# Batch 1's K and Q loaded and cast before the first feed-forward chunk, with a denser order for its attention

## The chip, the core and the metric

The kernel runs on one core of one Trainium2 chip. The time is the device time of one launch in microseconds; three runs of the kernel before gave 375.75 to 376.08, median 375.94. The engines are named as the profile names them: PE (TensorE, matrix products; PEld is its weight load), DVE (VectorE), ACT (ScalarE), POOL (GpSimd) and SP (SyncE, which here only issues DMAs). Each engine runs its own instructions in the order of the program and waits for the others by semaphores. ACTq and SPq in the profile are the sequencers of ACT and SP issuing DMAs.

## What is computed

Selective attention with a decay, then a feed-forward layer with a gate, in float32 from end to end in the reference:

```python
def _attn_ref(q, k, v, s) -> np.ndarray:
    B, H, S, D = q.shape
    scale = 1.0 / np.sqrt(D)
    scores = scale * np.matmul(q, k.transpose(0, 1, 3, 2))
    causal = np.triu(np.ones((S, S), dtype=bool), k=1)
    s_pos = np.maximum(s, 0.0)
    cum = np.cumsum(s_pos, axis=-1)
    bias = -(cum[:, :, :, None] - cum[:, :, None, :])
    scores = np.where(causal, -1000000000.0, scores + np.minimum(bias, 0.0))
    scores = scores - np.max(scores, axis=-1, keepdims=True)
    attn = np.exp(scores)
    attn = attn / (np.sum(attn, axis=-1, keepdims=True) + 1e-09)
    return np.matmul(attn, v).astype(np.float32)

def _moe_ref(x, w_gate, w_val, w_out, rms_g) -> np.ndarray:
    rms = np.sqrt(np.mean(x * x, axis=-1, keepdims=True) + 1e-06)
    xn = x / rms * rms_g
    g = xn @ w_gate
    silu = g * (1.0 / (1.0 + np.exp(-g)))
    val = xn @ w_val
    return (silu * val @ w_out).astype(np.float32)
```

Q, K and V have 8 batches, 8 heads, 576 rows and 64 columns; the gate, value and output weights are 512 x 1536, 512 x 1536 and 1536 x 512. The attention's output, 8 batches of 576 rows with 512 columns (8 heads of 64), is the input x of the feed-forward layer: 4608 tokens.

## The kernel before

**Feed-forward.** The 4608 tokens are cut into nine chunks of 512, whatever the batches; `ffn(c)` does one. For each of twelve blocks fb of 128 hidden columns, PE makes the gate product (L668, four matrix products into a bank psF), ACT takes the tanh of it into T (L671), PE makes the value product (L677), DVE makes U from T and the gate (L680) and one block later Ht from U and the value (L673; the last one is L685). Then four output tiles of twelve products each (L690) are copied by ACT (L695) and stored by SP (L697). psF has four buffers, T two.

**Attention.** A batch has nine score steps S(b, kb, g), key block kb of 128 keys, head group g of four heads (kb = 4 is the short last block with all eight heads), and ten value steps AV(b, qb, g), query block qb. Ahead of them K and Q must be cast to bf16 and be transposed:

- `load_kq` and `load_kq_tail` load K (w = 0) or Q (w = 1) of a batch into kq32, rows 0 to 511 and the last 64. kq32 is one buffer for each of K and Q, so the load of batch 1 waits for all casts of batch 0.
- `cast` writes part r of five (r = 4 is the tail) to kqn. For batch 2 and 3 the casts of both, from batch 4 on those of Q, are POOL's, planned by `casts`.
- `t_step` transposes two heads (hp) of K or Q on PE (L184) and copies the result to kqT, on ACT (L192) or DVE (L190); `tail_step` does the tails of all heads (L200, L205 to L209). From batch 2 on Q is transposed by DMA on SP (`kq_dma`, L171), from batch 4 on K too.
- `s_step` makes the scores on PE (L250) and their exponentials on ACT (L274), half of them in the next slot; POOL puts zeros above the diagonal (L283).
- `av_step` multiplies by V on PE (L300, L306), then DVE takes the reciprocal of the sums (L313) and scales (L315). With g = 1 the squares are summed, on DVE (L325) or ACT (L321), and POOL makes the row's factor in two instructions (L328, L331). g = 0 uses the bank psAV, g = 1 of batches from 1 on psT; there is one buffer of each.
- `x_scale` (L338, DVE) applies the factor three slots after AV(b, qb, 1). The result is transposed into xnT by DMA on SP (L348), or for batch 0 and for (1, 3) by PE (`xt_step`, L357, into psT).
- `check_mag` and `check_max` keep the largest magnitude of the cast K and Q (L369, then L375 for each half), for a test at the end which chooses between this path and a general one.

**Order.** There are no loops on the chip here; Python writes the instructions out in an order that it plans. A prologue, written by hand, does batch 0 up to query block 3 and ends with the transpose of x(0,3), which the first chunk needs. Every chunk then has 36 slots: `step()` is called after each gate group and each value group (slots 1 to 23), after the last Ht (24) and after each four output products (25 to 36). A slot takes at most one entry from each side queue (`act_side`, `pool_side`, `dve_side`; `v_side` in odd slots), all first in, first out, and then emits one S with a transpose of batch 1, or up to two of an x transpose, an AV and a transpose. `can_s`, `can_av`, `can_t` and `can_xt` say when, by the slots at which the inputs were emitted. In slots called bare, `pool_side` and `v_side` stand still; in chunk 0 these are 30 to 33.

`later(queue, lag, fns)` puts work into a side queue for `lag` slots ahead. For batch 1 the casts of K are in `act_side` and `pool_side`, those of Q in `dve_side` and `pool_side`. `check(0, (0,))` puts the check of batch 0's K into `dve_side`; its Q is checked in the prologue, after the last x transpose. The checks allow `casts(2)` to overwrite kqn.

The tokens of chunk 1 reach into batch 1, query block 3: x(1,3) is the last thing that chunk 1 waits for, and its transpose stands in chunk 0, in slot 34.

Of the kernel before, what the change touches and what calls it, by code (L numbers as in the profile page):

```python
# [26 lines left out]
def kernel(  # L27
# [76 lines left out]
    def psF16():  # L104
        return pp.tile([128, 8, 128], BF16, name="psF16", tag="F", bufs=4)
# [10 lines left out]
    def psT():  # L116
        return pp.tile([128, 8, 128], BF16, name="psT", tag="T", bufs=1)
# [5 lines left out]
    def load_kq(eng, b, w, h0=0, h1=H):  # L123
        src = k if w == 0 else q
        eng.dma_start(
            out=kq32[:, w, h0:h1, 0:256],
            in_=src[b, h0:h1, 0:512, :].rearrange("h (p r) d -> p h (r d)", r=4))

    def load_kq_tail(eng, b, w):
        src = k if w == 0 else q  # L130
        eng.dma_start(
            out=kq32[0:64, w, :, 256:320],
            in_=src[b, :, 512:576, :].rearrange("h p d -> p h d"))

    def cast(eng, b, w, r0, r1, h0=0, h1=H):
        o = kqn[:, b % 2, w, r0:r1, h0:h1, :]
        i = kq32[:, w].rearrange("p h (r d) -> p r h d", d=D)[:, r0:r1, h0:h1, :]
        if eng is nc.scalar:
            eng.activation(out=o, in_=i, func=AF.Copy)
        else:  # L140
            eng.tensor_copy(out=o, in_=i)
# [193 lines left out]
    def x_scale(b, qb):  # L335
        n = rows(qb)
        col = b * NSC + qb
        nc.vector.scalar_tensor_tensor(  # L338
            out=xs_sb[0:n, (b * NSC + qb) % NX, :], in0=x_sb[0:n, (b * NSC + qb) % NX, :],
            scalar=al_all[0:n, col:col + 1], in1=g_row[0:n], op0=ALU.mult, op1=ALU.mult)  # L340
# [68 lines left out]
    def later(queue, lag, fns):  # L409
        t = slot[0] + lag  # L410
        queue.extend((lambda: slot[0] >= t, f) for f in fns)
# [6 lines left out]
    def check(b, ws=(1, 0)):  # L418
        t = slot[0] + (8 if b >= KB else 0)

        def when(w):
            if b < 2:
                return slot[0] % 2 and chunk[0] == b
            return phase() >= 25 and slot[0] >= t and (w == 0 or ready(0, "cast", b, 1))
        dve_side.extend((lambda w=w: when(w), f) for w in (ws if b < KB else (0, 1)) for f in (
            lambda w=w: check_mag(b, w), lambda: check_max(0), lambda: check_max(1),
            lambda w=w: done.__setitem__(("check", b, w), slot[0])))

    def phase():

        return slot[0] - first[0]
# [57 lines left out]
    def do_t(key, **kw):  # L489
        b, hp, w = key  # L490
        if hp == "tail":
            tail_step(b)
            done["T", b] = slot[0]
            after_tail(b)
        else:
            if b == 1:
                kw["dve"] = w == 1 and hp > 1
                if hp % 2:
                    kw["pT"] = psF16()
            t_step(b, hp, w, **kw)  # L500
        done["T", b, hp, w] = slot[0]
        last["T"] = slot[0]
# [21 lines left out]
    def do_xt(key, pX=None):  # L524
        b, qb = key
        xt_step(b, qb, pX)
        done["XT", b, qb] = slot[0]
        last["T"] = slot[0]
# [13 lines left out]
    def can_s():  # L542
        if not s_seq or not slot_free():
            return False
        b, kb, g = s_seq[0]
        if b == 1 and (phase() < 24 and phase() % 2 == 0 or kb == 4 and at("AV", 1, 3, 1) > slot[0]):
            return False
        due = SLOTS * ((b * S + kb * 128) // DM) - (26 if b == 1 else 18 if b < 4 else 14)
        if slot[0] - last["S"] < (4 if slot[0] < due - 24 else 3 if slot[0] < due else 2):
            return False  # L550
        if b >= XB:
            return all(ready(5, "X", b, 1, c) for c in (kb, min(kb + 1, 4))) and (
                ready(5, "X", b, 0, kb) if b >= KB else ready(3, "T", b) if kb >= 3 else
                all(ready(3, "T", b, hp, 0) for hp in (2 * g, 2 * g + 1)))
        if kb >= 3 and not ready(3, "T", b):
            return False
        if kb == 4:
            return True
        return all(ready(3, "T", b, 2 * g + j, w) for j in (0, 1) for w in (0, 1))

    def can_av(clear=False):
        if not av_seq:
            return False
        b, qb, g = av_seq[0]
        if slot[0] - last["AV"] < (1 if (b, qb) == (1, 3) else 2):
            return False
        if b > 0 and g == 1 and slot[0] - last["T"] < 3 and not clear:
            return False
        if b > 1 and not ready(8, "V", b):
            return False  # L570
        if qb > 0 and not ready(5, "S", b, qb - 1, g):
            return False
        prev = b * NSC + qb - NX
        if prev >= 0 and at("XT", prev // NSC, prev % NSC) > slot[0]:
            return False
        return ready(4 if (b, qb) == (1, 3) else 5, "S", b, qb, g)
# [22 lines left out]
    def step(bare=False):  # L599

        slot[0] += 1
        while pending:
            pending.pop(0)()
        moved = False
        if scaled[0] < len(x_list):
            b, qb = x_list[scaled[0]]
            if ready(3, "AV", b, qb, 1):
                x_scale(b, qb)
                scaled[0] += 1
                if not by_pe(b, qb):  # L610
                    assert xt_seq[0] == (b, qb)
                    xt_dma(*xt_seq.pop(0))
                    done["XT", b, qb] = slot[0] + 4
                    moved = True
        run_side(act_side)
        if not moved and x_seq and slot[0] - last["X"] >= 2:
            b, w, c = x_seq[0]
            if (ready(2, "cast", b, 1) and ready(1, "S", b - 2, 4, 0)
                    and (w == 1 or ready(7, "K", b, c))):
                x_seq.pop(0)  # L620
                kq_dma(b, w, c)
                done["X", b, w, c] = last["X"] = slot[0]
                if b >= KB and (w, c) == (0, NSC - 1) and b + 2 < B:
                    casts(b + 2)
        bare = bare or chunk[0] == 0 and 30 <= phase() <= 33
        if slot[0] % 2 and not bare:
            run_side(v_side)
        if not bare:
            run_side(pool_side)
        run_side(dve_side)  # L630
        if can_s():
            pending.append(do_s(s_seq.pop(0)))
            if t_seq and t_seq[0][0] == 1 and can_t():
                do_t(t_seq.pop(0))
            return
        n = 0
        if can_xt():
            do_xt(xt_seq.pop(0))
            n += 1
        if can_av():  # L640
            do_av(av_seq.pop(0))
            n += 1
        if n < 2 and t_seq and can_t():
            do_t(t_seq.pop(0))
# [126 lines left out]
    with tc.manual_schedule():  # L771
# [28 lines left out]
        def piece(w, g, r, eng):  # L800
            cast(eng, 0, w, r, r + 1, 4 * g, 4 * g + 4)
# [4 lines left out]
        def s_first(kb, g, pair=None):  # L806
            do_s((0, kb, g), pair)()
# [25 lines left out]
        do_t((0, 3, 0), pT=psF16(), dve=True)  # L833
        for r in range(4):
            piece(1, 1, r, DVE)
        s_first(2, 0)
        for w in (0, 1):
            cast(POOL, 0, w, 4, 5)
        do_t((0, 2, 1), pT=psT(), dve=True)
        do_t((0, 3, 1), pT=psF16(), dve=True)  # L840
        do_av((0, 0, 0))
# [10 lines left out]
        s31 = do_s((0, 3, 1), pairF())  # L852
        s31(False)
        do_av((0, 0, 1), psT32())

        for w in (0, 1):
            nc.vector.memset(kq32[0:1, w, 0, 0:1], 0.0)
            load_kq(nc.sync, 1, w)
            load_kq_tail(nc.sync, 1, w)
        s30.mask()  # L860
        do_av((0, 1, 1), act=True)
        s31.mask()
# [14 lines left out]
        do_xt((0, 2), psF16())  # L877
        warm(2)
        x_scale(0, 3)
        do_xt((0, 3), psF16())  # L880
        check_mag(0, 1)
        check_max(0)
        check_max(1)
        done["check", 0, 1] = 0

        def done_cast(w):
            done["cast", 1, w] = slot[0]
        later(act_side, 1, [lambda r=r: cast(ACT, 1, 0, r, r + 1) for r in range(4)])
        later(pool_side, 1, [lambda: cast(POOL, 1, 0, 4, 5)])
        later(pool_side, 3, [lambda: done_cast(0)])  # L890
        later(pool_side, 4, [lambda: cast(POOL, 1, 1, 2, 3),
                             lambda: (cast(POOL, 1, 1, 3, 4), done_cast(1)),
                             lambda: cast(POOL, 1, 1, 4, 5)])
        later(dve_side, 3, [lambda r=r: cast(DVE, 1, 1, r, r + 1) for r in (0, 1)])
        later(v_side, 0, [
            lambda: load_v(1, 0), lambda: load_v(1, 1), lambda: load_v(1, 2),
            lambda: nc.gpsimd.dma_start(out=wout_sb,
# [2 lines left out]

        loads(2, 1, later, 14)
        loads(2, 0, later, 18)
        check(0, (0,))
        check(1)
        casts(2)

# [192 lines left out]
```

## Time and profile before

| what | value |
|---|---|
| three runs, median (range) | 375.94 us (375.75 to 376.08) |
| the profiled execution | 375.92 us, its span 374.2 us |
| granted clock of PE | 0.998 |
| first gate product of chunk 0, of chunk 1 | 32.12, 76.35 us |
| prologue's ACT, DVE and POOL busy, 20 to 30 us | 7.50, 6.83 and 6.56 of 10 us |
| first S of batch 1 (slot 11), first AV (slot 16) | 45.83, 52.46 us |
| AV(1,3,1) (slot 30), transpose of x(1,3) (slot 34) | 68.47, 74.15 us |
| load of batch 1's K, Q (rows 0 to 511): issue, to landing | 23.17 and 6.3; 24.35 and 9.0 us |

The span runs from the first to the last instruction; the time of the execution holds some 1.7 us more around it. All the times of single instructions are from the span's start. A row of a group has the line, the engine, the operation, the tile it writes and those it reads; x12 is a count; behind it stand the busy time, the mean length and the idle time of the engine ahead of it, with what ended that. Successive instructions of one engine overlap by up to 0.08 us in the records, so what an instruction costs its engine is the distance from its start to the next one's.

### The profile page before, as it was taken

What the parts mean: (1) busy time and instruction counts of PE and PEld (TensorE: products, weight loads), DVE (VectorE), ACT (ScalarE), POOL (GpSimd) and SP (SyncE); (2) the same over time, 40 slices, a digit from 0 to 9 for tenths busy, and PEclk for the clock granted to TensorE, in tenths of its full rate; (3) what the DMA queues carried; (4) which work ended last, traced back from release to release, by engine and by line L of the source; (5) the groups of instructions that cost most, each with busy time, mean ns of one, the idle gap of its engine ahead of it and who ended that gap; (6) DMA issues with size and microseconds to landing.
All of it is one profiled execution on the core that took longest, in us unless ns stands there. A gap on an engine that the chain in (4) does not pass through costs nothing. (4 is left out here: it accounts for less than half of the span.)

```text
span 374.2 us, 6937 instructions
## 1 busy us (share of the span) xinstructions
PE 347.0 (93%) x2356; PEld 161.4 (43%) x2356; DVE 279.7 (75%) x525; ACT 239.8 (64%) x626; POOL 174.4 (47%) x277
## 2 busy tenths in 40 slices
PE   1867899899999999899999999999999999999993
PEld 1443444454444444344444444444444444444441
DVE  6758988589887878788889897785488548837830
ACT  3777787547877597786777776777677744323321
POOL 5865734974846575779756825522322310000000
PEclk9999999999999999999999999999999999999999
DMA  8999999899997599959999997992210230020012
GB/s 230 189 227 237 146 196 220 123 204 225 155 168 105 53 195 165 159 55 204 149 162 225 136 107 152 120 67 44 96 26 14 44 105 3 0 84 31 0 44 76
DMA packets 125626, 46.22 MB, mean 124 GB/s; under 512 B 104912, under 2 KB 120784, under 8 KB 125584
## 3 DMA queue, kind: packets, MB, share of 16 engines
q0 software_dynamic: 59920, 11.80, 42.7%
q1 hardware_dynamic: 53040, 24.33, 34.6%
q10 hardware_dynamic: 12624, 9.59, 10.5%
q8 instruction: 20, 0.33, 0.4%
q14 instruction: 22, 0.18, 0.2%
HBM read 38.16 MB, written 9.44 MB: 127 GB/s over the span
## 5 line engine op out<-in xcount | busy, mean ns | idle before, releaser
L274 ACT ACTIVATE E<-psS,biasK 128x256 bf16<-128x256 f32 (+3 forms) x352 | 114.9, 415 | 19.7 <-PE psS L250 18.1
L668 PE MATMUL psF<-xnT,wg_sb 128*128 128x512 bf16 x432 | 111.1, 379 | 2.4 <-DMA xnT<-xs_sb 1.3
L677 PE MATMUL psF<-xnT,wv_sb 128*128 128x512 bf16 x432 | 111.1, 379 | 0.1
L690 PE MATMUL psF<-wout_sb,Ht 128*128 128x512 bf16 x432 | 102.3, 379 | 0.0
L283 POOL TENSOR_SCALAR_AFFINE_SELECT E<-E 128x512 bf16<-128x512 bf16 x72 | 52.2, 725 | 93.7 <-ACT E L274 92.8
L671 ACT ACTIVATE T<-psF 128x512 f32<-128x512 f32 x108 | 64.3, 597 | 42.1 <-PE psF L668 38.7
L680 DVE SCALAR_TENSOR_TENSOR U<-T,psF 128x512 bf16<-128x512 f32 x108 | 73.6, 682 | 21.9 <-ACT T L671 21.8
L673 DVE TENSOR_TENSOR Ht<-U,psF 128x512 bf16<-128x512 bf16 x99 | 67.7, 684 | 7.5 <-PE psS L250 0.5
L668 PEld LDWEIGHTS <-wg_sb 128*128 128x128 bf16 x432 | 38.7, 98 | 46.9 <-issue 8.0
L677 PEld LDWEIGHTS <-wv_sb 128*128 128x128 bf16 x432 | 38.6, 98 | 42.8 <-issue 4.6
L690 PEld LDWEIGHTS <-Ht 128*128 128x128 bf16 x432 | 38.7, 98 | 42.1 <-issue 2.3
L338 DVE SCALAR_TENSOR_TENSOR xs_sb<-x_sb,al_all,g_row 128x512 bf16<-128x512 bf16 (+1 forms) x40 | 32.8, 822 | 16.1 <-POOL al_all L331 14.5
L695 ACT ACTIVATE osb<-psF 128x512 f32<-128x512 f32 x36 | 21.4, 595 | 33.7 <-PE psF L690 29.4
L321 ACT ACTIVATE xs_sb<-x_sb 128x512 bf16<-128x512 bf16 (+1 forms) x36 | 22.9, 639 | 22.3 <-DVE x_sb L315 22.2
L175 POOL DMA_DIRECT2D v_sb<-in_v_dram x40 | 35.3, 883 | 0.4 <-issue 0.3
L375 DVE TENSOR_TENSOR acc<-acc,mag 128x1280 bf16<-128x1280 bf16 x32 | 29.4, 936 | 0.4
L250 PE MATMUL psS<-kqT 64*128 64x256 bf16 (+2 forms) x304 | 26.8, 262 | 1.6 <-ACT E L274 1.5
L306 PEld LDWEIGHTS <-E 128*128 128x128 bf16 x320 | 22.3, 99 | 13.3 <-POOL E L283 3.4
L328 POOL TENSOR_SCALAR al_all<-ss_all 128x1 f32<-128x1 f32 (+1 forms) x40 | 11.1, 277 | 28.5 <-ACT xs_sb L321 23.0
L300 PEld LDWEIGHTS <-E 128*128 128x128 bf16 x256 | 20.6, 99 | 7.9 <-DVE x_sb L315 0.6
L331 POOL TENSOR_TENSOR al_all<-al_all,mhalf 128x1 f32<-128x1 f32 (+1 forms) x40 | 22.2, 556 | 3.3
L250 PEld LDWEIGHTS <-kqT 64*128 64x128 bf16 x320 | 10.4, 97 | 29.9 <-issue 28.6
(94 smaller groups left out, 278.8 us busy)
## 6 DMA issues: line engine op xcount, KB each, us to landing
out_dram<-osb SPq DMA_DIRECT2D x36, 256.0 KB, 2.3
kq<-in_q_dram ACTq DMA_DIRECT2D x6, 1024.0 KB, 9.5
v_sb<-in_v_dram POOLq DMA_DIRECT2D x32, 128.0 KB, 7.2
kq<-in_k_dram ACTq DMA_DIRECT2D x2, 1024.0 KB, 10.6
kqn<-in_k_dram POOLq DMA_DIRECT2D x16, 128.0 KB, 5.6
wg_sb<-in_moe_w_gate_dram POOLq DMA_DIRECT2D x2, 768.0 KB, 7.3
wv_sb<-in_moe_w_val_dram POOLq DMA_DIRECT2D x2, 768.0 KB, 10.3
wout_sb<-in_moe_w_out_dram POOLq DMA_DIRECT2D x1, 1536.0 KB, 14.1
```

The source lines that it names most:

```text
L175: nc.gpsimd.dma_start(out=v_sb[0:n, b % 2, c, :, 0:64], in_=v[b, :, c * 128:c * 128 + n, :].rearrange("h p d -> p h d"))
L250: nc.tensor.matmul(pair[par][:, j * W:j * W + M], lhsT=kT, rhs=qT, start=(j == 0), stop=(j == nj - 1))
L274: nc.scalar.activation(out=eo, in_=ei, func=AF.Exp, scale=0.125, bias=biasK[:, kb, bh:bh + 1])
L283: nc.gpsimd.affine_select(out=Ev[:, :, 0:nq], in_=Ev[:, :, 0:nq], pattern=[[0, nh], [1, nq]], compare_op=ALU.is_ge, fill=0.0, base=0, chan ...
L338: nc.vector.scalar_tensor_tensor(out=xs_sb[0:n, (b * NSC + qb) % NX, :], in0=x_sb[0:n, (b * NSC + qb) % NX, :], scalar=al_all[0:n, col:col ...
L375: nc.vector.tensor_tensor(out=acc[:, sl], in0=acc[:, sl], in1=mag[:, sl], op=ALU.max)
L668: nc.tensor.matmul(Gp, lhsT=wg_sb[:, cc, fs], rhs=xnT[:, cc, x0:x0 + DM], start=(cc == 0), stop=(cc == CC - 1))
L671: nc.scalar.activation(out=T, in_=Gp, func=AF.Tanh, scale=0.5)
L673: nc.vector.tensor_tensor(out=Ht[:, fb - 1, :], in0=pend[0], in1=pend[1], op=ALU.mult)
L677: nc.tensor.matmul(Vp, lhsT=wv_sb[:, cc, fs], rhs=xnT[:, cc, x0:x0 + DM], start=(cc == 0), stop=(cc == CC - 1))
L680: nc.vector.scalar_tensor_tensor(out=U, in0=T, scalar=1.0, in1=Gp, op0=ALU.add, op1=ALU.mult)
L690: nc.tensor.matmul(Op, lhsT=Ht[:, fb, tb * 128:(tb + 1) * 128], rhs=wout_sb[:, fb, :], start=(fb == 0), stop=(fb == FB - 1))
```

## The change

It concerns batch 1 and the checks of batch 0:

- The loads of batch 1's K and Q are issued by SP some way earlier in the prologue: the main parts behind the DVE casts of batch 0's Q, the tails behind POOL's casts of batch 0's tails.
- At the end of the prologue, K is cast in two parts by DVE and two by ACT, Q in four parts by DVE. The two tails stay on POOL, in slots 1 and 4. The casts that POOL, ACT and DVE had in slots 1 to 4 are gone, and the planner is told that the casts are done (slot -1).
- The prologue no longer checks batch 0's Q: both checks of batch 0 are in `dve_side`, from slot 9 on.
- The copies of all Q transposes of batch 1 are DVE's; those of the first two were ACT's.
- S of batch 1 may come every second slot from the start (`due` is 36 slots ahead, not 26). AV of batch 1 may follow one slot after another from slot 22 on; before, that was so for query block 3 alone.
- The bare slots of chunk 0 are 27 to 30.

```diff
@@ def check(b, ws=(1, 0)) @@
             if b < 2:
-                return slot[0] % 2 and chunk[0] == b
+                return slot[0] % 2 and chunk[0] == b and slot[0] >= 9
@@ def do_t(key, **kw) @@
             if b == 1:
-                kw["dve"] = w == 1 and hp > 1
+                kw["dve"] = w == 1
@@ def can_s() @@
-        due = SLOTS * ((b * S + kb * 128) // DM) - (26 if b == 1 else 18 if b < 4 else 14)
+        due = SLOTS * ((b * S + kb * 128) // DM) - (36 if b == 1 else 18 if b < 4 else 14)
@@ def can_av(clear=False) @@
-        if slot[0] - last["AV"] < (1 if (b, qb) == (1, 3) else 2):
+        if slot[0] - last["AV"] < (1 if b == 1 and slot[0] > 21 else 2):
@@ def step(bare=False) @@
-        bare = bare or chunk[0] == 0 and 30 <= phase() <= 33
+        bare = bare or chunk[0] == 0 and 27 <= phase() <= 30
@@ the prologue @@
         for r in range(4):
             piece(1, 1, r, DVE)
+        for w in (0, 1):
+            DVE.memset(kq32[0:1, w, 0, 0:1], 0.0)
+            load_kq(nc.sync, 1, w)
         s_first(2, 0)
         for w in (0, 1):
             cast(POOL, 0, w, 4, 5)
+            load_kq_tail(nc.sync, 1, w)
...
-        for w in (0, 1):
-            nc.vector.memset(kq32[0:1, w, 0, 0:1], 0.0)
-            load_kq(nc.sync, 1, w)
-            load_kq_tail(nc.sync, 1, w)
         s30.mask()
...
         x_scale(0, 3)
+        cast(DVE, 1, 0, 2, 3)
+        cast(DVE, 1, 0, 3, 4)
+        cast(ACT, 1, 0, 0, 1)
         do_xt((0, 3), psF16())
-        check_mag(0, 1)
-        check_max(0)
-        check_max(1)
-        done["check", 0, 1] = 0
-
-        def done_cast(w):
-            done["cast", 1, w] = slot[0]
-        later(act_side, 1, [lambda r=r: cast(ACT, 1, 0, r, r + 1) for r in range(4)])
+        cast(ACT, 1, 0, 1, 2)
+        for r in range(4):
+            cast(DVE, 1, 1, r, r + 1)
+        done["cast", 1, 0] = done["cast", 1, 1] = -1
         later(pool_side, 1, [lambda: cast(POOL, 1, 0, 4, 5)])
-        later(pool_side, 3, [lambda: done_cast(0)])
-        later(pool_side, 4, [lambda: cast(POOL, 1, 1, 2, 3),
-                             lambda: (cast(POOL, 1, 1, 3, 4), done_cast(1)),
-                             lambda: cast(POOL, 1, 1, 4, 5)])
-        later(dve_side, 3, [lambda r=r: cast(DVE, 1, 1, r, r + 1) for r in (0, 1)])
+        later(pool_side, 4, [lambda: cast(POOL, 1, 1, 4, 5)])
...
-        check(0, (0,))
+        check(0)
         check(1)
```

## The prediction

> **What bounds the kernel now.** I read first the page's busy row and the table of windows.
>
> ```profile
> PE 347.0 (93%) x2356; PEld 161.4 (43%) x2356; DVE 279.7 (75%) x525; ACT 239.8 (64%) x626; POOL 174.4 (47%) x277
> ...
> 34.30:63.75 29.45, 27.49 (x217) 13.09 (x216) 26.29 (x51) 23.71 (x58) 13.20 (x21) 1.00 1.24 190
> 63.75:76.35 12.60, 11.11 (x96) 5.54 (x94) 6.84 (x17) 5.89 (x19) 11.27 (x19) 1.00 0.90 143
> ```
>
> PE is the bound over the whole span, at full clock (1.00). But the change touches chunk 0 only, 32.12 (first L668) to 76.35 (chunk 1's first L668), and there it reads differently: between VectorE's first U (34.30) and its last Ht (end 63.75) DVE is busy 26.29 of 29.45 us; after that it has room, and POOL is full (11.27 of 12.60). (A row of windows: stretch and its length, busy us and instructions of PE, PEld, DVE, ACT, POOL, clock, DMA share, GB/s.) The chain of waits names only the last store (L695), so it says nothing here. The waits of PE in 32 to 76.4 us do:
>
> ```profile
> PE psT L357 <- DVE xs_sb L338: 1.5, 1, 1.5
> PE psT L184 <- ACT kqn L139: 1.1, 1, 1.1
> PE psF L668 <- ACT xnT L364: 0.7, 1, 0.7
> PE psT L184 <- POOL kqn L141: 0.5, 1, 0.5
> ```
>
> The 0.7 lies before the first L668; 3.1 us are batch 1's: transposes that wait for their casts (1.1 and 0.5), and the transpose of x(1,3) near the chunk's end (1.5). The timelines of PE and POOL (start, length, instruction) show the last:
>
> ```profile
> 71.64 1.03 PE L690 MATMUL psF<-wout_sb,Ht 128*128 128x512 bf16 x4
> 74.15 0.40 PE L357 MATMUL psT<-ident_bf,xs_sb 128*128 128x128 bf16 x4 [1.49 <-DVE xs_sb L338]
> ...
> 71.07 0.95 POOL L175 DMA_DIRECT2D v_sb<-in_v_dram  x1
> 72.09 0.18 POOL L328 TENSOR_SCALAR al_all<-ss_all 128x1 f32<-128x1 f32 x1
> 72.36 0.57 POOL L331 TENSOR_TENSOR al_all<-al_all,mhalf 128x1 f32<-128x1 f32 x1
> ```
>
> The squares of (1,3) ended at 70.31 on ACT, but its factor ran at 72.09: POOL was behind with a V load and casts. So 3.1 us is the prize. The question is what else holds chunk 0 once it is gone.
>
> **The new calendar, by the planner's rules.** Steps are slots 1 to 36 of chunk 0. With both casts marked -1, the eight transposes go to slots 1 to 8, the tail to 9. S(1,0,0) needs its four transposes three slots back: slot 7 (11 before), then one S every odd slot to 21. AV(0,4) stays at 8 and 10, x(0,4) at 16. AV(1,0,0) goes to 12; (1,0,1) stays at 20, since x(0,4) uses psT at 16; then (1,1,0) 22, (1,1,1) 23 (24 before), (1,2,0) 24, (1,2,1) 25, (1,3,0) 26, (1,3,1) 27 (30 before). x(1,3) is transposed at 31 (34), AV(1,4) at 33 and 34 (36, 38). The checks of batch 0, six passes, take slots 9, 11, 13, 17, 19, 21; three of them ran ahead of chunk 0 before.
>
> **Prologue: nothing.** The K and Q loads move up behind the DVE casts that end at 15.36; SyncE issues nothing else until 62.39, so its longer waits hold up nobody. K landed at 29.47 (issue 23.17 and 6.3), Q at 33.40 (24.35 and 9.0); issued some 8 us sooner they land at best that much sooner, at worst as before if the weight loads in flight keep them off. The ACT casts of K take 0.62 each and fall into two gaps of ACT, 0.87 before L364 at 31.47 and 1.11 before the first tanh at 33.18; without those gaps each would push the first L668 by 0.54. On DVE six casts at 0.34 from start to start (36.10, 36.44) are 2.0 us where check_mag and check_max took 3.40 (30.90 to 34.30), so U(0) starts at its tanh's end, 33.8, not 34.3. Were Q as late as before, the casts would end near 34.8, and U(0) waits behind them; DVE's idle time in slots 1 to 6 (1.8 us, below) takes that up.
>
> **Chunk 0: DVE.** Start to start U, Ht and a kqT copy take 0.60 each (duration 0.68, next start 0.08 before its end).
>
> ```profile
> L680 DVE SCALAR_TENSOR_TENSOR U<-T,psF 128x512 bf16<-128x512 f32 x12 | 8.1, 678 | 1.0 <-ACT T L671 1.0
> L673 DVE TENSOR_TENSOR Ht<-U,psF 128x512 bf16<-128x512 bf16 x11 | 7.5, 679 | 0.8 <-PE psS L250 0.5
> L190 DVE COPY kqT<-psF 128x512 bf16<-128x512 bf16 x1 | 0.7, 678 | 0.0
> L375 DVE TENSOR_TENSOR acc<-acc,mag x32: 807/820/2270, 32.4 to 230.9; 128x1280 bf16<-128x1280 bf16 x32
> ```
>
> Up to the fourth U PE sets the pace: 4 gate and 3 value groups at 0.86 (32.12 to 32.98), 7 transposes at 0.22, S(0,4) 0.32 and S(1,0,0) 0.42 with the 0.10 lost before each, then tanh and one kqT copy bring the end of U(3) to 42.05 (42.29 before); DVE idles 1.8 us in there. From then DVE has, up to the last Ht: 8 U 4.8, 9 Ht 5.4, one kqT copy 0.6, the tail's copy 0.3, three AVs without squares at 0.55 and three with at 1.27 (42.43 to 42.98, 44.91 to 46.18) 5.5, two x_scale at 0.67 1.3, one x copy 0.2, six checks at 0.74 4.4, and 0.18 in each of three places where Ht directly follows its U (55.01 to 55.12) 0.5. Sum 23.1. PE's own work between the same points is 18.9 us (16 groups 13.8, seven S at 0.42 2.9, transposes 0.9, AV 1.3), and PE can run ahead only by the four psF buffers, so DVE never idles again. Before, from 42.29 to 63.75, it was 21.5 with 1.5 of idle.
>
> A pass that meets POOL is stretched. The timelines of DVE and POOL side by side:
>
> ```profile
> 88.22 0.82 DVE L375 TENSOR_TENSOR acc<-acc,mag 128x1280 bf16<-128x1280 bf16 x1
> ...
> 90.35 2.27 DVE L375 TENSOR_TENSOR acc<-acc,mag 128x1280 bf16<-128x1280 bf16 x1
> ...
> 89.50 0.89 POOL L175 DMA_DIRECT2D v_sb<-in_v_dram  x1
> 90.39 1.17 POOL L149 CAST kqn<-kq 128x512 bf16<-128x512 f32 x2
> 91.50 0.89 POOL L175 DMA_DIRECT2D v_sb<-in_v_dram  x1
> ```
>
> Eleven passes of this kind (checks, squares, scales) stand in the stretch. Bounds: nothing, or 0.26 each as in batch 0's own three checks (3.23 us for 2.46), 2.9. In 45 to 62 us, where POOL runs masks and few loads as it will here, one of four squares and scales was stretched (1.04 for 0.69), 0.09 each: I take 1.0. The last Ht then ends at 42.05 + 23.1 + 1.0 = 66.15 (65.1 to 68.0), 2.4 later than before.
>
> The Trainium skill, "SBUF — State Buffer", section "Who interferes with whom", states that a VectorE instruction that needs the port pair shared with GpSimd blocks until a running GpSimd instruction ends, and the other way round. The 2.27 against 0.82 agrees; with POOL busy 13.20 of 29.45 us and half a mask (0.63) as the wait, the rule alone would make the eleven passes 11 x 0.45 x 0.32 = 1.6 dearer, an estimate, and the whole 377.9.
>
> What follows it: AV(1,3,0) reuses psAV, so it waits for DVE's two operations on AV(1,2,0), which stand behind the last Ht: 0.65, and 0.1 to PE. From there PE has 40 L690 at 0.216 (8.64), S(1,4,0) 0.32, x(1,3) 0.23 and four AV halves at 0.25: 10.2. x(1,3) itself no longer waits: in slots 27 to 30 POOL gets neither casts nor V loads, so the factor follows the squares at once; if POOL were as late as before, the 1.5 would come back. Chunk 1 begins at 66.15 + 10.95 = 77.1 for 76.35: **+0.75**. AV(1,4,1) is no longer in chunk 1: **-0.25**.
>
> **Chunk 1: POOL and SyncE.** The quiet slots 27 to 30 push two casts of batch 2's Q and two V loads to slots 31 to 33, ahead of K's four casts (34 to 37), and AV(1,4,1) at slot 34 puts its factor among them. Counted from slot 31: load 0.95, two casts 1.1, load 0.95, cast 0.6; then the factor waits for the squares until 4.9 and ends at 5.65; load, two casts, load, cast 3.6, and 0.5 to 0.9 where casts stretch (1.05 at 73.52): 9.75 to 10.15. PE reaches the first transpose of batch 2 (slot 41) after ten groups, x(1,3) and two AVs: 9.4. A wait of 0.35 to 0.75 where 2.3 was to spare (K's last of four casts 78.57, transpose 80.91): **+0.6**, bounds 0 and 1.2. SyncE: the second transposing load of batch 2's Q moves from slot 33 to 38, behind x(1,4), which waits for that factor; issued at 7.8 from slot 31 (factor 5.65, scale 0.75, 1.4 to issue x(1,4)), with 5.8 to landing (issue 75.15) or 9.1 (issue 77.41), it lands at 13.6 to 16.9; S(2,0,0) comes at 15.1 (9.4, the wait 0.6, five groups and three transposes). **+0.3**, bounds 0 and 1.8.
>
> Sum: +0.75 - 0.25 + 0.6 + 0.3 = +1.4 us. The profiled execution took 375.92 (span 374.2 and 1.7 around it; the median is 375.94): **377.3**. Put as one line, the change is H - 64.75, where H is the end of chunk 0's last Ht.
>
> **Rivals.** *Faster: DVE is not the pace.* If PE paces chunk 0 its groups add up to 144 x 0.216 = 31.1, transposes 2.7, AV 2.7, S 4.0: 40.5 us for 44.2, so -3.75 - 0.25 + 0.6 = 372.5. For it: DVE kept up before. Against it: 26.29 of 29.45, and the change adds three checks, two kqT copies and AV(1,1,1) with its squares (2.2 + 1.2 + 1.3), and takes away two casts (0.7). It decides where H falls under 64.0; my list has 65.1 without any stretch. 0.28. *No change:* chunk 0 as worked out, but batch 2's transposes and S find their inputs ready: 376.4. For it: the bounds of 0. 0.14. *The early loads collide:* K and Q ahead of the gate weights (landed 19.70, read by the fillers at 23.76) and of V(0,3) (20.71, read at 24.62) would put these off by 7.9 us (3.9 lie between K's landing and Q's), AV(0,3,1) from 27.12 to 28.9 and the first L668 with it: +1.8, 379.1. Against it: a load that ACT issued at 49.50 behind the output weights needed 11.7 us where SyncE's took 9.0, so it waited instead of going first. 0.08.
>
> **Numbers.** The forecast has 0.50, its own range 376.2 to 379.4 (H from 65.1 to 68.0, and not all bounds of chunk 1 at once). A measurement here tells 0.2% (0.75 us) from nothing; faster 0.28, same 0.14, slower 0.58. To leave out no more than two tenths the range reaches into the faster rival: 373.6 to 379.2.
>
> **What would show it.** Right: no wait of L184 for kqn in chunk 0; the wait of L357 gone; DVE without idle time from 41 to 66; PE waits for DVE (U, rZ or Ht's line) in 50 to 67; the last Ht near 66, chunk 1 at 77.1; L184 waiting for POOL's cast at about 81. Wrong: a last Ht before 64.7, the first L668 away from 32.1, or chunk 1 starting near 73.

## The result and the profile after

| what | before | after |
|---|---|---|
| runs of one comparison, median (range) | 376.08 us (375.36 to 377.09, 9) | 377.37 us (377.05 to 379.26, 9) |
| ratio | | 1.0048, 95% interval 1.0033 to 1.0064 |
| profiled execution, its span, clock | 375.92, 374.2, 0.998 | 377.05, 375.8, 0.995 |
| first L668 of chunk 0, of chunk 1 | 32.12, 76.35 | 32.31, 76.46 |
| last Ht of chunk 0 (H) | 63.75 | 65.69 |
| length of chunk 1 | 39.17 | 40.80 |
| chunks 2 and 3 together | 78.66 | 77.96 |
| end of the last L690 | 368.21 | 369.24 |

By the ratio, which weighs all runs, the change makes the kernel slower by 0.48%; the two medians differ by 1.29 us. The traces show one execution each, for the kernel after the shortest of its nine. Between these two the loss lies in chunk 1 (+1.63 us). Chunks 4 to 8 have the same lengths in both traces.

Busy times on the page of the kernel after are 3.0 us higher for PE, which keeps its share, and 2.5 for DVE:

```profile
PE 350.0 (93%) x2356; PEld 162.5 (43%) x2356; DVE 282.2 (75%) x531; ACT 237.6 (63%) x622; POOL 173.5 (46%) x275
```

The waits of PE in 32 to 76.4 us, kernel after (engine, tile, line, releaser: us in total, times, longest):

```profile
PE psAV L300 <- DVE x_sb L315: 1.6, 2, 1.4
PE psF L668 <- ACT xnT L364: 0.7, 1, 0.7
PE psT L300 <- DVE x_sb L315: 0.5, 1, 0.5
PE psS L250 <- ACT E L274: 0.3, 1, 0.3
PE psF L668 <- DVE U L680: 0.2, 1, 0.2
```

The waits of 3.1 us that were the prize are gone: no L184 waits for a cast, no L357 for the scale. In their place PE waits for DVE; the longest wait, 1.4, is that of AV(1,3,0) for the bank psAV, right behind H. The table of windows of the kernel after (columns as before: length, busy us of PE, PEld, DVE, ACT, POOL, clock, DMA share, GB/s), from U(0) to H and from H to chunk 1:

```profile
35.40:65.69 30.29, 28.16 (x225) 13.15 (x224) 28.93 (x58) 21.00 (x54) 14.82 (x21) 1.00 1.11 190
65.69:76.46 10.77, 10.16 (x84) 5.20 (x85) 6.10 (x17) 5.49 (x17) 6.94 (x14) 1.00 0.60 113
```

DVE is busy 28.93 of 30.29 us, so chunk 0 takes as long as before (44.15 for 44.23). Chunk 1 is another matter. First PE's timeline there (start, length, instruction, and in brackets the idle time before it with its releaser):

```profile
79.05 1.03 PE L677 MATMUL psF<-xnT,wv_sb 128*128 128x512 bf16 x4
81.55 1.02 PE L668 MATMUL psF<-xnT,wg_sb 128*128 128x512 bf16 x4 [1.47 <-DVE U L680]
82.41 0.39 PE L184 MATMUL psT<-ident_bf,kqn 128*128 128x128 bf16 x4
```

The third gate product waits for the first U, the transpose behind it (L184) for nobody. In the kernel before, DVE made the first U at once and the scale of (1,4) much later:

```profile
78.04 0.69 DVE L680 SCALAR_TENSOR_TENSOR U<-T,psF 128x512 bf16<-128x512 f32 x1
...
81.93 0.74 DVE L338 SCALAR_TENSOR_TENSOR xs_sb<-x_sb,al_all,g_row 64x512 bf16<-64x512 bf16 x1
```

DVE's timeline in the kernel after says why U is late:

```profile
77.27 2.89 DVE L338 SCALAR_TENSOR_TENSOR xs_sb<-x_sb,al_all,g_row 64x512 bf16<-64x512 bf16 x1 [1.71 <-POOL al_all L331]
80.09 0.81 DVE L369 TENSOR_SCALAR mag<-kqn 128x2560 uint16<-128x2560 uint16 x1
80.83 0.67 DVE L680 SCALAR_TENSOR_TENSOR U<-T,psF 128x512 bf16<-128x512 f32 x1
```

`x_scale(1, 4)` stands ahead of U in DVE's order. It waits 1.71 us for POOL's factor and then takes 2.89 us where it took 0.74 before; the check pass behind it (L369) puts U off by 0.74 more. POOL's timeline beside it:

```profile
76.41 0.18 POOL L328 TENSOR_SCALAR al_all<-ss_all 64x1 f32<-64x1 f32 x1 [1.22 <-ACT xs_sb L321]
76.68 0.56 POOL L331 TENSOR_TENSOR al_all<-al_all,mhalf 64x1 f32<-64x1 f32 x1
77.20 0.94 POOL L175 DMA_DIRECT2D v_sb<-in_v_dram  x1
78.15 1.17 POOL L141 CAST kqn<-kq 128x512 bf16<-128x512 f32 x2
79.26 2.13 POOL L175 DMA_DIRECT2D v_sb<-in_v_dram  x1
81.38 1.17 POOL L141 CAST kqn<-kq 128x512 bf16<-128x512 f32 x2
```

The scale ends 0.84 us after the two casts do (80.16 and 79.32), so it seems to have got through only behind POOL's load and casts; the next V load in its turn took 2.13 us for 0.89. U starts at 80.83; in the kernel before it started at 78.04, at the end of its tanh.

### The profile page after: what moved, and what is told of

Read it like the earlier page. It is cut to its first block, busy times and chain, and to the rows that moved or that the text cites. A ratio compares the mean times of both kernels' runs of the same rounds, so it can differ in the third digit from the quotient of the medians.

```text
span 375.8 us, 6938 instructions
## 1 busy us (share of the span) xinstructions
PE 350.0 (93%) x2356; PEld 162.5 (43%) x2356; DVE 282.2 (75%) x531; ACT 237.6 (63%) x622; POOL 173.5 (46%) x275
## 4 chain that ended last, share of the span: by engine, by line
PE 66%; DVE 12%; DMA 8%; POOL 5%; ACT 4%; issue 3%; POOLq 0%; ACTq 0%; DVEq 0%
PE psF L690 22%; PE psF L668 18%; PE psF L677 18%; DMA kq<-in_q_dram 5%; PE psS L250 4%; DVE U L680 2%; DVE xs_sb L338 2%; ACT E L274 2%; DVE Ht L673 2%; DMA kqT<-kqn 2%; DVE acc L375 2%; DVE x_sb L315 1%; DMA kq<-in_k_dram 1%; POOL v_sb L175 1%; POOL E L283 1%
## 5 line engine op out<-in xcount | busy, mean ns | idle before, releaser
L668 PE MATMUL psF<-xnT,wg_sb 128*128 128x512 bf16 x432 | 111.1, 379 | 3.4 <-DVE U L680 1.9
L690 PE MATMUL psF<-wout_sb,Ht 128*128 128x512 bf16 x432 | 102.3, 379 | 0.0
L668 PEld LDWEIGHTS <-wg_sb 128*128 128x128 bf16 x432 | 38.8, 98 | 48.1 <-issue 9.4
L690 PEld LDWEIGHTS <-Ht 128*128 128x128 bf16 x432 | 38.7, 98 | 41.9 <-issue 2.1
L338 DVE SCALAR_TENSOR_TENSOR xs_sb<-x_sb,al_all,g_row 128x512 bf16<-128x512 bf16 (+1 forms) x40 | 34.3, 860 | 15.5 <-POOL al_all L331 15.5
L375 DVE TENSOR_TENSOR acc<-acc,mag 128x1280 bf16<-128x1280 bf16 x32 | 27.9, 883 | 0.3
L306 PEld LDWEIGHTS <-E 128*128 128x128 bf16 x320 | 23.0, 101 | 11.8 <-POOL E L283 2.0
L328 POOL TENSOR_SCALAR al_all<-ss_all 128x1 f32<-128x1 f32 (+1 forms) x40 | 11.9, 298 | 32.3 <-ACT xs_sb L321 25.3
L300 PEld LDWEIGHTS <-E 128*128 128x128 bf16 x256 | 21.0, 101 | 11.3 <-DVE x_sb L315 4.3
```

Of the source, the lines that this page charges most:

```text
L338: nc.vector.scalar_tensor_tensor(out=xs_sb[0:n, (b * NSC + qb) % NX, :], in0=x_sb[0:n, (b * NSC + qb) % NX, :], scalar=al_all[0:n, col:col ...
L375: nc.vector.tensor_tensor(out=acc[:, sl], in0=acc[:, sl], in1=mag[:, sl], op=ALU.max)
L668: nc.tensor.matmul(Gp, lhsT=wg_sb[:, cc, fs], rhs=xnT[:, cc, x0:x0 + DM], start=(cc == 0), stop=(cc == CC - 1))
L690: nc.tensor.matmul(Op, lhsT=Ht[:, fb, tb * 128:(tb + 1) * 128], rhs=wout_sb[:, fb, :], start=(fb == 0), stop=(fb == FB - 1))
```

## The experiments

All of them are edits of the kernel after; a ratio is always to the kernel before, run beside it. The last table of this section has the numbers of all their traces. U(3) is chunk 0's fourth U, H the end of its last Ht.

### What sets chunk 0

`a_no_check0` leaves out the six check passes of batch 0: the test of its magnitudes is not made.

```diff
-            lambda w=w: check_mag(b, w), lambda: check_max(0), lambda: check_max(1),
+            lambda w=w: b and check_mag(b, w), lambda: b and check_max(0), lambda: b and check_max(1),
```

> The changed kernel without the six passes that check batch 0's K and Q (left out: that part of the range test). Theory, DVE paces chunk 0: the end of the last Ht (H, 65.7 with the passes) falls by up to 6 x 0.74 = 4.4 us, until PE's own work paces; chunk 0 falls from 44.15 to 40.5 to 41.5 us; of the 3 us some 1 to 1.5 may come back in chunk 1, so the time is 1.5 to 3.5 below the changed kernel's. Rival, chunk 0 is paced by PE, ACT or POOL: H and chunk 0 stay within 0.5 us and the time within 0.5.

The ratio is 1.0016 (1.0005 to 1.0027). H came at 64.56, chunk 0 took 43.11 us, not the 40.5 to 41.5 of the theory: DVE lost 4.9 us of passes, and the chunk became 1.0 us shorter. From the end of U(3) to H it is 21.76 us instead of 23.31. The groups of DVE between these points, first the kernel after, then this one, show where the rest went (busy us, mean ns, and idle us ahead of the group with its releaser):

```profile
L680 DVE SCALAR_TENSOR_TENSOR U<-T,psF 128x512 bf16<-128x512 f32 x9 | 6.1, 677 | 0.0
```

```profile
L680 DVE SCALAR_TENSOR_TENSOR U<-T,psF 128x512 bf16<-128x512 f32 x9 | 6.1, 679 | 1.4 <-ACT T L671 1.4
...
L209 DVE COPY kqT<-psT 128x256 bf16<-128x256 bf16 x1 | 0.3, 293 | 0.8 <-ACT kqT L207 0.8
```

Without the passes U waits for its tanh: PE and ACT are the pace for a part of the way, 1.55 us under DVE's. PE's last value group starts at 60.59 in the kernel after and at 60.61 here: up to there the passes hardly hold PE up. They pile up on DVE, and PE waits for DVE almost only behind that group.

`e_kcheck_late` keeps all passes and puts the three for K behind H, to slots 25, 27 and 29.

```diff
-                return slot[0] % 2 and chunk[0] == b and slot[0] >= 9
+                return slot[0] % 2 and chunk[0] == b and slot[0] >= (9 if w or b else 25)
```

> The changed kernel with the three check passes of batch 0's K at slots 25, 27 and 29, behind the last Ht, instead of 17, 19 and 21. Theory: PE sets chunk 0 up to its last value group (start 60.59 in the changed kernel, 60.61 without any check), and only what DVE then still has ahead of the last Ht counts; Q's three passes (44 to 51 us) are taken up by DVE's idle time, K's (54.45, 56.57, 59.79) are not. So all of the 1.1 us that leaving out all six gave comes from these three: last Ht at 64.6, chunk 1 at 75.4, time 1.0 under the changed kernel's 377.37: 376.4. Rival, the prediction's sum (DVE is the pace, every pass costs the like, 1.13 / 6 = 0.19): last Ht at 65.1, time 376.8. Second rival: the passes delay x(1,3) or an AV behind the last Ht, chunk 1 starts more than 10.9 after it, nothing gained.

H fell to 64.39 (22.14 behind U(3)), but chunk 1 started 12.34 us after it instead of 10.77, and the ratio is 1.0059 (1.0035 to 1.0083): the second rival. POOL's timeline shows how the passes delay x(1,3):

```profile
67.37 1.23 POOL L331 TENSOR_TENSOR al_all<-al_all,mhalf 128x1 f32<-128x1 f32 x1
...
69.86 0.99 POOL L331 TENSOR_TENSOR al_all<-al_all,mhalf 128x1 f32<-128x1 f32 x1
```

In the kernel after both take 0.55. DVE's passes ran at just these times:

```profile
67.38 0.81 DVE L375 TENSOR_TENSOR acc<-acc,mag 128x1280 bf16<-128x1280 bf16 x1
...
69.63 0.82 DVE L375 TENSOR_TENSOR acc<-acc,mag 128x1280 bf16<-128x1280 bf16 x1
```

`i_passes_spread` puts K's passes to slots 15, 17 and, behind the scale of x(1,3), 31.

```diff
-                return slot[0] % 2 and chunk[0] == b and slot[0] >= 9
+                return (slot[0] % 2 or i == 3 and b < 1) and chunk[0] == b and slot[0] >= (31 if i == 2 and w + b < 1 else 9)
```

(i counts the four entries of a check: three passes and the mark that it is done.)

> The changed kernel with batch 0's passes for Q at slots 9, 11, 13, for K at 15, 17 and the last at 31, behind the scale of x(1,3); AV(1,4) stays where the change puts it. Theory: a pass counts only if it stands between the last value groups and the last Ht, so moving two passes a few slots up and one behind frees what leaving out all six freed: last Ht 32.0 to 32.4 after the first gate product (33.4 in the changed kernel, 32.3 without passes), no wait of L357 (1.2 in the run with K's passes at 25 to 29), chunk 0 43.1, chunk 1 as in the changed kernel 40.8 to 41.0, time 376.4. Rival, DVE's sum: five of six passes still ahead of the last Ht, so it ends at 33.2 and the time is 377.2.

Chunk 0 took 43.35 us and L357 waited for nothing, but H lay 22.72 behind U(3), between the two theories, and part of the gain was an early U(3): the 0.59 us between fit the one pass that went behind H and leave nothing for the two that moved up. So the place of these two ahead of H did not matter. My theory of a few bad places fell, and the prediction's sum stands, as far as PE's pace lets it. The time did not fall (1.0052, 1.0026 to 1.0078). In this trace chunk 1 is 0.55 us longer than in the kernel after (S(2,0,0) waits 1.0 for a transposing load) and chunk 4 1.89, as its waits show (all engines, 208 to 216 us):

```profile
DVE xs_sb L338 <- POOL al_all L331: 2.6, 1, 2.6
...
PE psF L677 <- DVE Ht L673: 1.9, 1, 1.9
POOL kqn L149 <- DVE U L680: 1.7, 1, 1.7
```

A scale that waits for POOL stands ahead of an Ht again. POOL itself waited for a cast of batch 5's Q, and the DVE named there had long been done: the load landed at 211.34, the cast began at 211.46. That load was issued 1.95 us late, at 197.99, just after a transposing load into kqT had landed at 197.93; it then took 13.35 us, against 9.14 in the kernel after.

### What lost the time in chunk 1

`b_loads_late` puts the loads of batch 1's K and Q back to their old place, behind `do_av((0, 0, 1), psT32())`.

```diff
-        for w in (0, 1):
-            DVE.memset(kq32[0:1, w, 0, 0:1], 0.0)
-            load_kq(nc.sync, 1, w)
...
         do_av((0, 0, 1), psT32())
+        for w in (0, 1):
+            DVE.memset(kq32[0:1, w, 0, 0:1], 0.0)
+            load_kq(nc.sync, 1, w)
+            load_kq_tail(nc.sync, 1, w)
```

> The changed kernel with the loads of batch 1's K and Q back at their old place in the prologue. Theory, the DMA engines are full until 33 us and the order of the queues decides little: K lands near 29.5 and Q near 33.4, the last cast of Q ends within 0.5 us of 35.5, and the time stays within 0.5 us. Rival, the earlier loads are what lets the casts stand in the prologue: the casts of Q and the first U come 1 us or more later and the time rises by 0.5 to 1.5.

1.0049 (1.0036 to 1.0062), the same as the kernel after: the sooner loads bought nothing. Their issues in the kernel after, in SP's timeline:

```profile
15.68 0.37 SPq L125 DMA_DIRECT2D kq<-in_k_dram  x1
16.22 0.47 SPq L125 DMA_DIRECT2D kq<-in_q_dram  x1
17.13 7.74 SPq L131 DMA_DIRECT2D kq<-in_k_dram  x1
```

and their rows among its DMA issues (count, KB each, us from issue to landing):

```profile
kq<-in_k_dram SPq DMA_DIRECT2D x1, 1024.0 KB, 13.0
kq<-in_q_dram SPq DMA_DIRECT2D x1, 1024.0 KB, 16.9
```

Issued 7.5 and 8.1 us sooner, they landed 0.8 and 0.2 us sooner (28.64 and 33.17), and the issue of K's tail took 7.74 us.

`c_bare_30` sets the bare slots of chunk 0 back to 30 to 33.

```diff
-        bare = bare or chunk[0] == 0 and 27 <= phase() <= 30
+        bare = bare or chunk[0] == 0 and 30 <= phase() <= 33
```

> The changed kernel with the bare slots back at 30 to 33. Theory, POOL's backlog after slot 31 makes chunk 1 longer: two casts and two V loads run before slot 30 again, x_scale of (1,4) is not stretched to 2.9 us, and chunk 1 falls from 40.8 by 1 to 1.6 us; in exchange the factor of (1,3) stands behind POOL's work and PE waits 0.5 to 1.5 at the transpose of x(1,3), so the time is within 1 us. Rival, the bare slots decide neither: chunk 1 stays at 40.8 within 0.3 and no wait of L357 appears.

1.0079 (1.0066 to 1.0092). The wait of L357 is back (1.0), chunk 1 starts 11.98 us after H: the new place of the bare slots is worth 1.2 us in chunk 0. Chunk 1 is as long as with them moved (41.02), so their push on POOL's casts is not what makes it long.

`d_av14_late` puts AV(1,4) where it was before the change.

```diff
+        if (b, qb) == (1, 4) and slot[0] < (36, 38)[g]:
+            return False
```

> The changed kernel with AV(1,4,0) and AV(1,4,1) back at slots 36 and 38. Theory, the factor of (1,4) among POOL's casts and the x_scale of (1,4) ahead of chunk 1's first U are what holds chunk 1: its first U starts at the tanh's end (about 78) and not at 80.8, the 1.6 us wait of L668 for U goes, and the time falls by 1 to 1.5 us. Rival, POOL's casts of batch 2's K hold PE as soon as U does not: the first transpose of batch 2 waits for them (L184 for POOL) and the gain is under 0.5.

1.0028 (1.0013 to 1.0043). The scale of (1,4) now comes behind the first U, which starts 1.69 us after chunk 1 does, at the end of its tanh, instead of 4.36; chunk 1 takes 39.05 us. But this moves the factor in POOL's order as well. `j_xscale_held` leaves POOL's order as it is and holds the scale (with x(1,4)'s transposing load, which is issued behind it):

```diff
-            if ready(3, "AV", b, qb, 1):
+            if ready(3, "AV", b, qb, 1) and ((b, qb) != (1, 4) or slot[0] >= 40):
```

> The changed kernel with x_scale(1,4) alone held until slot 40, behind chunk 1's second U; POOL's order, AV(1,4) and all the rest stay. Theory: chunk 1's loss of 1.6 is this instruction standing ahead of the first U while it waits for the factor and then for POOL's port: first U at 78 to 79, no wait of the third gate product for U (1.5 now), chunk 1 39.2 to 39.9, time 376.2. Rival, the prediction's own link (POOL's casts of K behind the factor, late for batch 2's first transposes): POOL's order is unchanged, K's last of four casts still ends at 82.0 when PE comes at 80.9, so L184 waits 1.1 for POOL and chunk 1 stays near 40.3, time 376.9.

0.9977 (0.9968 to 0.9986), 375.24 us: faster than before the change. Chunk 1 takes 38.65 us. DVE's timeline in this run:

```profile
75.94 0.81 DVE L369 TENSOR_SCALAR mag<-kqn 128x2560 uint16<-128x2560 uint16 x1
78.60 0.69 DVE L680 SCALAR_TENSOR_TENSOR U<-T,psF 128x512 bf16<-128x512 f32 x1 [1.86 <-ACT T L671]
...
81.33 1.05 DVE L338 SCALAR_TENSOR_TENSOR xs_sb<-x_sb,al_all,g_row 64x512 bf16<-64x512 bf16 x1
```

U waits for nothing but its tanh, and the scale takes 1.05 us. The check pass that stood between the scale and U now runs ahead of both, while DVE would be idle. A transposing load of batch 2's Q is issued sooner too (78.21 for 81.46), but S(2,0,0) waits 0.2 for it in both kernels. POOL's order is the same as in the kernel after, but its timeline is not:

```profile
78.59 1.17 POOL L141 CAST kqn<-kq 128x512 bf16<-128x512 f32 x2
79.70 0.89 POOL L175 DMA_DIRECT2D v_sb<-in_v_dram  x1
80.59 1.25 POOL L141 CAST kqn<-kq 128x512 bf16<-128x512 f32 x2
```

The V load is back at 0.89, so K's casts come just in time for L184 at 81.22. The rival, which had POOL late whatever DVE does, fell.

### What can be put together

`f_kcheck_av14` is e and d in one, `g_f_squares_act` has the squares of x(1,1) on ACT besides, `h_f_loads_late` is f with the loads at the old place.

```diff
-        act = act or b > 1 or b == 1 and qb > 1
+        act = act or b > 1 or b == 1 and qb > 0
```

> The same, and AV(1,4,0) and AV(1,4,1) at slots 36 and 38, where they were before the change. Theory: the two losses are apart and add up: chunk 0 43.1, chunk 1 39.05 (first U at its tanh's end), chunk 2 39 to 40; PE's last product ends near 366.5, the median 1.0 under that of the run with late AV(1,4) alone (376.79): 375.8, its best runs at 374.5. Rival: what chunk 0 gains comes back in chunk 2, whose first gate product waits for a transposing load (1.3 in the kernel before): median 376.8, PE's wait for xnT near 1.5.

> The same again, with the squares of x(1,1) on ACT instead of DVE. Theory: these squares (0.69) stand right ahead of the last U on DVE while PE waits, so the last Ht ends 0.6 sooner, at 64.0, and the time falls by 0.6. Rival: PE's last value group and the tanh behind it are the limit, or ACT with the squares puts off the last tanh: last Ht at 64.5 or later, no gain.

> The second kernel of this group with the loads of batch 1's K and Q at their old place. Theory: the sooner loads bought nothing (K landed at 28.64 instead of 29.47), so first gate product and median are those of the second kernel within 0.4 us. Rival: the sooner loads share the DMA engines with the weights and make the runs scatter (375.4 to 378.1 with them, 377.1 to 378.1 without): without them the runs lie within 1 us and the median falls by 0.7 or more.

f: 1.0017 (1.0000 to 1.0035); g: 1.0023 (1.0005 to 1.0040); h: 1.0029 (1.0003 to 1.0056). H lies 22.15, 21.41 and 22.16 behind U(3), so the squares are worth 0.7 there, as their 0.69 says; but the wait of L357 (1.2 in each) takes the gain as it did in e, and in f and h S(2,0,0) waits 1.3 and 0.9 for batch 2's transposing load. The loads make no difference again, and h's runs scatter no less than f's.

`k_i_av14_act_loads` joins i, d, the squares on ACT and the late loads; `l_held_spread` joins i and j.

> All that helped at once: passes spread as in the first of this group, AV(1,4) at slots 36 and 38, squares of x(1,1) on ACT, loads at the old place. Theory: first gate product 32.1, chunk 0 42.9, chunk 1 39.05, chunks 2 and 3 together 78.0 to 78.6, PE's last product ends at 366.3, time 374.2: 0.35% under the kernel before. Rival: what chunk 0 gains comes back before chunk 4 as waits for transposing loads (S(2,0,0) for kqT 0.9 to 1.3 in two runs of the last group), the median stays within 0.2% of the kernel before.

> x_scale(1,4) held until slot 40 and batch 0's passes spread (Q at 9, 11, 13, K at 15, 17, 31), nothing else against the changed kernel: the two losses taken out at once. Theory: chunk 0 43.35, chunk 1 38.65 to 39.1, chunks 2 and 3 together 78.0, chunk 4 37.73: PE's last product at 366.2, time 374.0 to 374.4, 0.5% under the kernel before. Rival: chunk 0's gain is given back in chunk 4, where batch 5's Q load is issued late behind a transposing load (1.95 and 1.37 in the two runs that had a short chunk 0) and POOL's factor and PE wait for it: chunk 4 39.0 to 39.6, time 375.2 to 376, no better than with x_scale held alone (375.24).

k: 0.9998 (0.9982 to 1.0015), the rival's time, but not by its waits: chunk 0 took 42.82 us, but chunk 1 39.83, where gate products wait 0.9 for U, and chunk 4 39.18, in a trace in which the issue of batch 5's Q load waited 2.77 us. l: 0.9981 (0.9971 to 0.9991), 375.10 us. Chunk 4 kept its 37.73, yet l is no better than j: its chunk 0 is 0.70 us shorter than j's (43.91 for 44.61), but its chunk 1 0.65 longer (39.30 for 38.65), with two waits that j does not have, 0.2 of L184 for POOL's cast and 0.4 of a gate product for U. So what chunk 0 gave came back as waits in chunk 1.

The traces (times in us; the number of runs in each comparison was 5 to 12):

| kernel | ratio | U(3) end | U(3) to H | H to chunk 1 | chunk 1 | chunks 2, 3 | chunk 4 | last L690 |
|---|---|---|---|---|---|---|---|---|
| before | 1 | 42.29 | 21.46 | 12.60 | 39.17 | 78.66 | 37.73 | 368.21 |
| after | 1.0048 | 42.38 | 23.31 | 10.77 | 40.80 | 77.96 | 37.73 | 369.24 |
| a | 1.0016 | 42.80 | 21.76 | 10.77 | 41.03 | 78.49 | 39.02 | 370.15 |
| b | 1.0049 | 42.38 | 23.31 | 10.77 | 41.03 | 77.96 | 37.73 | 369.46 |
| c | 1.0079 | 42.41 | 23.31 | 11.98 | 41.02 | 77.95 | 37.73 | 370.70 |
| d | 1.0028 | 42.67 | 23.32 | 10.53 | 39.05 | 77.96 | 37.73 | 367.54 |
| e | 1.0059 | 42.25 | 22.14 | 12.34 | 41.03 | 78.42 | 37.73 | 370.19 |
| f | 1.0017 | 42.91 | 22.15 | 12.10 | 40.07 | 77.96 | 37.73 | 369.20 |
| g | 1.0023 | 43.09 | 21.41 | 12.31 | 39.02 | 78.26 | 37.99 | 368.37 |
| h | 1.0029 | 41.93 | 22.16 | 12.10 | 39.67 | 78.22 | 38.43 | 368.80 |
| i | 1.0052 | 42.08 | 22.72 | 10.78 | 41.35 | 78.00 | 39.62 | 370.83 |
| j | 0.9977 | 42.81 | 23.32 | 10.78 | 38.65 | 77.95 | 37.73 | 367.52 |
| k | 0.9998 | 42.54 | 21.99 | 10.53 | 39.83 | 77.98 | 39.18 | 368.33 |
| l | 0.9981 | 42.65 | 22.71 | 10.77 | 39.30 | 77.94 | 37.73 | 367.38 |

The column from U(3) to H is the cleanest: 23.31 or 23.32 in each of the five kernels with all six passes ahead of H, 22.7 with five, 22.15 with three, 21.76 with none.

## Why the prediction came out

The forecast was 377.3, the median 377.37. That they are so close is luck: chunk 0 lost 0.64 us less than the sum has, chunk 1 lost 0.98 more, and 0.70 came off chunks 2 and 3, for which it has nothing. And one loss was put to the wrong link.

| term, against the kernel before | predicted | measured |
|---|---|---|
| chunk 1's start: U(3) end | -0.24 | +0.09 |
| DVE's work from there to H | +2.64 | +1.85 |
| from H to chunk 1 | -1.65 | -1.83 |
| together | +0.75 | +0.11 |
| length of chunk 1 | +0.65 | +1.63 |
| chunks 2 and 3 | 0 | -0.70 |
| behind the last L690 | 0 | +0.10 |
| sum | +1.4 | +1.13 |

(The kernel before has 42.29, 21.46 and 12.60 for the first three; the last row but one is 375.92 - 368.21 = 7.71 and 377.05 - 369.24 = 7.81.)

**DVE is the pace of chunk 0: right.** Its list of work gave 23.1 us nominal, and 23.31 is what five traces show. Of the stretch of 1.0 only some 0.2 came (one scale of 0.96 for 0.74), so the passes hardly met POOL in this part. The prediction's estimate from the rule of the Trainium skill ("SBUF — State Buffer", section "Who interferes with whom") was 1.6, too much.

**Rival "faster, PE paces": rightly put behind, but wrongly priced.** It counted on H falling far below 64; without any pass H still comes 21.76 us after U(3). What DVE's passes hide is 1.55 us, not 3.75. A sum of one engine's work has no tail in it: behind PE's last value group (60.61 in a) U, Ht and the attention's scaling still follow one another up to H at 64.56.

**Prologue: the bad end of what was said.** Nothing for the first gate product was near (+0.19). K and Q landed nearly as late as before, and two of Q's four casts took 0.83 and 0.85 instead of 0.42, while POOL ran a cast and a V load: U(0) started at 35.40, not 33.8. DVE's idle time did not take up all of it, and U(3) ended 0.33 later than worked out. The rival with the early loads in the way fell: the gate weights landed at 19.40 and V(0,3) at 22.22, for 19.70 and 20.71, not 7.9 later.

**The wait of L357 goes: right**, and c shows that it goes by the bare slots.

**Chunk 1: the size was off, and the link.** The step that failed is "POOL's casts late for batch 2's first transposes: +0.6". The prediction had the factor of (1,4) among K's casts on POOL, and saw who waits for the casts, but not that the scale which waits for this factor stands ahead of chunk 1's first U on DVE. j shows that this, with the check pass that it kept waiting, is the loss: holding the scale takes chunk 1 from 40.80 to 38.65. POOL's casts are next in line, as l's chunk 1 hints (L184 waits 0.2 for them). The wait of S(2,0,0), +0.3, measured 0.2 (but 1.3, 1.0 and 0.9 in f, i and h); the -0.25 for AV(1,4,1) holds: d, which has it in chunk 1 again, takes 0.24 us less from H to chunk 1.

**Chunks 2 and 3: not foreseen.** Chunk 3's first gate product waited 1.3 us for a transposing load before and 0.6 after. The kernel before has one trace here; the thirteen of the kernel after and its edits have 77.9 to 78.5 us for the two chunks together, but whether the change did this is open.

**Open too** is why the medians of a, d, f, h, i and k lie 1.1 to 1.35 us over their shortest runs, those of j and l only 0.6 and 0.5. The load of batch 5's Q may be one source. In the traces of a, g, h, i and k its issue waits 0.8 to 2.8 us, each time until a transposing load into kqT lands, and in just these five chunk 4 is longer than 37.73; in the other nine it does not wait. No run here takes this wait away, so that it is the cause is not shown.

## What to carry to other kernels

When a stall is removed, ask first which engine was nearly full in that stretch: chunk 0 gave back 3.1 us of waits to a DVE that was 89% busy. An operation that must wait for a slow engine is placed behind what the bounding engine needs next: one scale moved by three slots took 2.15 us off chunk 1 and the ratio from 1.0048 to 0.9977, more than any other single edit. Measure a step between two events in the trace (U(3) to H) rather than by the total time; there 0.6 us is plain, in the total it drowns.

## What the hardware showed

Two engines that are each on time can hold each other up: the scale took 2.89 us beside POOL's load and casts, and POOL's next load 2.13 for 0.89 beside the scale and the check; in e a factor on POOL took 1.23 for 0.55 beside a check pass. The rule of the Trainium skill named above ("SBUF — State Buffer", section "Who interferes with whom"), that the two share a port pair and one blocks while the other holds it, agrees in kind. But it speaks of one instruction, and here the scale ended only behind three of POOL's in a row.

Sooner issues did not mean sooner data here: K and Q took 13.0 and 16.9 us from issue to landing, where the same loads took 6.3 and 9.0 when issued 7.5 and 8.1 us later.
